# A spectral mixer in fp32 on one core: the first pair of token tiles of a feature phase is combined before it is turned and turned in 32x32 squares, and sums, weight steps and second-layer weights stand at other places

## The chip, the core and the metric

The kernel runs on one core of a Trainium2 chip. Each core has TensorE for matmuls (PE; its weight loads are PEld), VectorE (DVE), ScalarE (ACT), GpSimd (POOL) and SyncE (SP), which here issues nearly all DMAs. Each engine works through its own instructions in order and waits on semaphores for the others. The metric is the device time of one execution in microseconds (us). The kernel before takes 2624.86 us, the median of three runs (2624.60 to 2625.03).

## What is computed

Two layers, each of a Fourier mixing and an MLP, both behind a layer norm, on 2048 tokens of 576 features, all in fp32:

```python
S, D, F = 2048, 576, 4608
def _A_ref(x, dft_seq_re, dft_seq_im, dft_hid_re, dft_hid_im):
    a = jnp.einsum("bsd,ed->bse", x, dft_hid_re)
    b = jnp.einsum("bsd,ed->bse", x, dft_hid_im)
    return jnp.einsum("ts,bse->bte", dft_seq_re, a) - jnp.einsum("ts,bse->bte", dft_seq_im, b)
def _B_ref(x, w1, b1, w2, b2):
    y = _layernorm(x, axis=-1)
    h = _gelu(jnp.einsum("bsd,df->bsf", y, w1) + b1)
    return jnp.einsum("bsf,fd->bsd", h, w2) + b2
x = A_x
x = x + _A_ref(_layernorm(x, axis=-1), ...)
x = x + _B_ref(_layernorm(x, axis=-1), B_w1, B_b1, B_w2, B_b2)
x = x + _A_ref(_layernorm(x, axis=-1), ...)
x = x + _B_ref(_layernorm(x, axis=-1), B_w1, B_b1, B_w2, B_b2)
```

## The kernel before, in words

**Parts and products.** An fp32 matrix is kept as two parts, a rounded high part (a ScalarE copy) and the difference to it, the low part (a VectorE or GpSimd subtraction). A product of two such matrices is three matmuls, high by high, high by low and low by high (`PASSES`), all issued in `mm` (L211). Large products are made of seven block products in place of eight (Winograd's scheme), which asks for sums and differences of blocks of both operands ahead of them and of the results behind.

**A layer** is a sequence phase (`Sequence`) and two halves, each of a feature phase (`hidden`) and an MLP (`mlp`), for 8 token tiles of 128 at a time. So there are four feature phases; the first is that of layer 0, half 0, and is the only one whose feature matrix is not yet split (`made` is false).

**Sequence phase.** A tile t of output (14 of them, two more are made ahead) is seven steps, one for each block product, 24 matmuls of 288 columns each. Around step n, written in one loop (`run`): VectorE makes the low part of step n+2 (`low`), with two updates of blocks in place; ScalarE makes the high part of step n+3; behind the matmuls of step n come its sums out of the accumulators (`post`), and at the last step VectorE turns the result in squares (L208). `sums(t + 1)` adds two blocks into a spare one and updates a third in place for the next tile; it stands at n % 7 = 2. The blocks come by DMA (in_cs, 512 KB) into a ring of six, so block 3 of tile t+1, one of the two that `sums` adds first, is loaded when block 0 of tile t is given back in the first step of tile t.

**Weights in the background.** In layer 0 a generator (`weights`) splits the first-layer weights: ScalarE's high parts (L284, L285), VectorE's low part (128 x 3 x 128), GpSimd's differences of blocks, and a store. `pump` runs one piece of it. `run` pumps twice a step, but for step 2 of a tile; the MLP of the first half goes on at the places in `BEHIND`. The generator is finished in that half.

**Feature phase.** For n = 0 to 7: 54 matmuls, whose first operand is token tile n, loaded, and split by `turn(n)` a step ahead. VectorE adds the result to the tile (L198), the layer norm's statistics follow (L226 to L234, with a power function on GpSimd, L232), and ScalarE normalizes (L238, L258) into a slot of two tiles (`t8`), a pair j. For pairs 0, 1 and 2, behind n = 2, 4 and 6, `rests` copies the remainder of the columns (L977), and `turn_blocks` turns four blocks on TensorE: 8 transposes (L991) and 4 of the remainders (L994), with two ScalarE copies out of the accumulators (L995, L996). In the step behind, `turn_sums` makes the first parts (L1004 and differences) and four differences of the turned blocks, `turn_parts` the parts of those, all into the MLP's operand `y`. The last pair is summed unturned, and `turn_y` turns its seven blocks on TensorE.

**MLP.** 18 chunks of 49 wide matmuls (`inner`), in groups of two; behind each chunk from group 1 on, a part of the second product of the group before (`outer`, 96 or 72 matmuls). A chunk accumulates in four banks, and the next one in the other four. In the first half of layer 0 the second-layer weights are made on the way (`make`): for each group a list of steps at due places, `soon` in the group and `late` in the next one. `advance` runs what is due after each block product, and the pumps.

## Time and profile before

| | us |
|---|---|
| median of three runs | 2624.86 |
| the profiled execution, its own time | 2624.75 |
| its span in the profile | 2623.0 |
| TensorE busy | 2614.4 |
| VectorE busy | 1836.8 |
| ScalarE busy | 1120.2 |
| GpSimd busy | 791.5 |

The page gives the busy time of each engine. Groups of instructions are named by line, engine, operation and tiles, with count, busy time, and mean duration in ns of one. A row of the timeline starts with its start in us and its length; "x4" is the number of instructions merged in it, and what stands in brackets is the engine's idle time ahead, with the instruction that ended it. A row of the chain that ended last has start, length, and engine with line. In a table of stretches a row is a stretch of the span with its length, the busy time of PE, PEld, DVE, ACT and POOL in it with the number of instructions, the granted clock, the busy share of the DMA engines and GB/s.

### The profile page before, as it was taken

The page shows a single profiled execution, that of the slowest core. Times are in us where ns is not written, and L with a number is a line of the kernel's source. Part 1 is how long each engine was busy: PE and PEld are TensorE (multiplying, and loading weights), DVE is VectorE, ACT ScalarE, POOL GpSimd, SP SyncE. Part 2 cuts the span into 40 slices and gives each one's busy share as a digit, 9 for nine tenths or more (in the row PEclk, how much of TensorE's full clock was granted, in tenths as well). Part 3 has the DMA queues.
Part 4 walks back from the last instruction along what each step waited for, and adds up shares of the span by engine and source line. Part 5 has one row for each costly group of instructions (what it writes and reads, how often), then busy time and mean ns, then how long its engine had stood idle before and what let it go on. Part 6 is the DMA issues. An engine that isn't in the chain of part 4 may idle for free.

```text
span 2623.0 us, 44794 instructions
## 1 busy us (share of the span) xinstructions
PE 2614.4 (100%) x17252; PEld 2466.3 (94%) x17252; DVE 1836.8 (70%) x2580; ACT 1120.2 (43%) x1821; POOL 791.5 (30%) x638
## 2 busy tenths in 40 slices
PE   9999999999999999999999999999999999999999
PEld 9999999899999989998999999999999999899998
DVE  8999987778787765556687776576555557655555
ACT  7555555555553443333354333353333325433332
POOL 5334333544444332222251000132122233322222
PEclk9999999999999999999999999999999999999999
DMA  6667676778788666676544343756666685666664
GB/s 226 223 236 234 234 255 215 266 278 301 279 299 300 178 202 195 194 222 210 173 175 135 122 124 124 211 159 194 193 195 194 195 268 169 199 195 195 194 194 155
DMA packets 223238, 544.91 MB, mean 208 GB/s; under 512 B 23712, under 2 KB 74912, under 8 KB 222880
## 3 DMA queue, kind: packets, MB, share of 16 engines
q1 hardware_dynamic: 210496, 513.91, 62.2%
q10 hardware_dynamic: 12528, 28.12, 2.8%
q8 instruction: 137, 2.24, 0.3%
q14 instruction: 77, 0.63, 0.1%
HBM read 429.87 MB, written 114.72 MB: 208 GB/s over the span
## 4 chain that ended last, share of the span: by engine, by line
PE 92%; DVE 5%; DMA 1%; issue 1%; POOL 1%; ACT 0%; DVEq 0%; ACTq 0%; SPq 0%; POOLq 0%
PE bank L211 91%; DVE R L201 3%; DVE A L201 1%; DMA w_parts<-R 1%; DMA A<-in_cs 0%; PE bank L991 0%; DVE A L198 0%; PE bank L1035 0%; DVE moments L242 0%; PE bank L994 0%; ACT R L698 0%; DMA A<-in_w 0%; DMA R<-w_parts 0%; PE bank L1045 0%; POOL A L198 0%
## 5 line engine op out<-in xcount | busy, mean ns | idle before, releaser
L211 PE MATMUL bank<-R 128*128 128x288 f32 (+2 forms) x16972 | 2585.9, 314 | 3.9 <-DVE R L201 1.2
L211 PEld LDWEIGHTS bank<-R 128*128 128x128 f32 x16972 | 2434.8, 189 | 150.8 <-DVE R L201 4.3
L198 DVE TENSOR_TENSOR A<-bank,A 128x576 f32<-128x576 f32 (+3 forms) x812 | 567.6, 707 | 510.2 <-PE bank L211 457.7
L201 POOL TENSOR_TENSOR R<-A,R 128x512 fp32r<-128x512 f32 (+1 forms) x292 | 380.0, 1310 | 912.4 <-ACT R L1299 560.6
L201 DVE TENSOR_TENSOR R<-A,R 128x1024 fp32r<-128x1024 f32 (+10 forms) x534 | 535.0, 1028 | 34.6 <-ACT R L698 14.3
L1299 ACT ACTIVATE R<-A 128x512 fp32r<-128x512 f32 x288 | 177.5, 630 | 356.4 <-DVE A L201 219.5
L198 POOL TENSOR_TENSOR A<-A 128x576 f32<-128x576 f32 (+2 forms) x102 | 155.0, 1527 | 531.1 <-ACT A L743 338.9
L1234 ACT ACTIVATE bank<-bank,b1t 128x512 f32<-128x512 f32 (+1 forms) x224 | 144.9, 647 | 350.5 <-DVE bank L198 233.6
L698 ACT ACTIVATE R<-A 128x1024 fp32r<-128x1024 f32 x196 | 205.6, 1054 | 123.8 <-PE bank L211 61.0
L198 DVE TENSOR_TENSOR bank<-bank,A 128x512 f32<-128x512 f32 (+1 forms) x228 | 152.3, 670 | 147.7 <-PE bank L211 147.0
L201 POOL TENSOR_TENSOR A<-A 128x288 f32<-128x288 f32 (+3 forms) x152 | 190.3, 1255 | 198.1 <-DVE R L201 103.6
L201 DVE TENSOR_TENSOR A<-A 128x1024 f32<-128x1024 f32 (+3 forms) x166 | 163.5, 989 | 6.2
L201 DVE TENSOR_TENSOR R<-bank,R 128x512 fp32r<-128x512 f32 x232 | 156.1, 676 | 5.5 <-ACT R L1299 5.0
L1299 ACT ACTIVATE R<-bank 128x512 fp32r<-128x512 f32 x216 | 121.0, 595 | 33.9 <-PE bank L211 33.9
L201 DVE TENSOR_TENSOR A<-bank,A 128x512 f32<-128x512 f32 x144 | 98.1, 681 | 0.4
L1261 ACT ACTIVATE A<-bank 128x512 f32<-128x512 f32 (+1 forms) x76 | 43.7, 575 | 120.2 <-PE bank L211 120.1
L284 ACT ACTIVATE R<-A 128x256 fp32r<-128x256 f32 x126 | 51.9, 412 | 63.7 <-DMA w_parts<-R 27.1
L1234 ACT ACTIVATE A<-bank,b1t 128x512 f32<-128x512 f32 (+1 forms) x76 | 50.5, 665 | 63.4 <-DVE bank L198 63.4
L232 POOL TENSOR_TENSOR moments<-moments,power 128x1 f32<-128x1 f32 x32 | 25.5, 797 | 134.9 <-DVE moments L234 117.5
L285 ACT ACTIVATE R<-A,power,middle 128x128 fp32r<-128x128 f32 x126 | 60.6, 481 | 0.0
L258 ACT ACTIVATE A<-A,moments 128x576 f32<-128x576 f32 x58 | 49.3, 867 | 23.7 <-DMA A<-x_mid 11.7
L198 DVE TENSOR_TENSOR A<-A 128x1024 f32<-128x1024 f32 x28 | 35.8, 1277 | 20.0 <-DMA A<-in_cs 12.3
(70 smaller groups left out, 612.9 us busy)
## 6 DMA issues: line engine op xcount, KB each, us to landing
R<-w_parts SPq DMA_DIRECT2D x504, 320.0 KB, 3.4
R<-w_parts SPq DMA_DIRECT2D x189, 576.0 KB, 3.7
A<-in_cs SPq DMA_DIRECT2D x112, 512.0 KB, 4.5
w_parts<-R SPq DMA_DIRECT2D x63, 576.0 KB, 6.2
w_parts<-R ACTq DMA_DIRECT2D x75, 320.0 KB, 4.3
w_parts<-R SPq DMA_DIRECT2D x51, 320.0 KB, 4.9
uv_mid<-A SPq DMA_DIRECT2D x28, 576.0 KB, 5.4
A<-in_w SPq DMA_DIRECT2D x72, 192.0 KB, 5.4
```

What stands on the lines that cost most here:

```text
L198: engine.tensor_tensor(dst, a, b, op=op)
L201: engine.tensor_tensor(dst, a, b, op=OP.subtract)
L211: nc.tensor.matmul(o, a, b, start=start, stop=stop, skip_group_check=True)
L232: nc.gpsimd.tensor_tensor(mv[:, 3:4], mv[:, 2:3], power[:, 0:1], op=OP.pow)
L258: nc.scalar.activation(dst, src, AF.Identity, bias=mv[:, 4:5], scale=mv[:, 3:4])
L284: nc.scalar.activation(t[:, 1:4:2], src[:, 0:3:2], AF.Copy)
L285: nc.scalar.activation(t[:, 2], src[:, 1], AF.Identity, bias=power[:, 2:3], scale=middle)
L698: nc.scalar.activation(self.cells[t, i](2, NP, P)[:, 0], self.source(t, i), AF.Copy)
L1234: nc.scalar.activation(dst, src, AF.Gelu_apprx_tanh, bias=bias(f))
L1261: nc.scalar.activation(up, o, AF.Copy)
L1299: nc.scalar.activation(H[q, k](2, TC)[:, 0], src, AF.Copy)
```

## The change

It has three parts. In the sequence phase, `sums` is taken apart: the addition stands at step 3, the update at step 4, and the step without pumps is step 6; in the last tile pumps go on for longer. In the first MLP half, the first four steps of group 0's `late` list move into group 0 (`due` at 5, 6, 12 and 13), `BEHIND` has other places, and group 1 has its own list with two pumps less (`BEHIND_1`). And in the three later feature phases (`flip`) the first pair is not turned by TensorE: ScalarE normalizes it into a mixed order of columns (`mixed`), VectorE makes the four differences unturned and turns all seven blocks in squares of 32 (`turn_first`), `move_first` writes them to DRAM (`y_mid`) and reads them back with the squares at their places, and `first_parts` makes the parts late in step 4.

```diff
--- before.py
+++ after.py
@@ -62,7 +62,9 @@
 EXTRA_AT = 7424
 EARLY_X = (12800, 9344, 8192)
 EARLY_T = 10496
-BEHIND = (0, 2, 2, 4, 5, 6, 15, 16, 16, 17, 17, 19, 21, 21)
+BEHIND = (0, 2, 4, 4, 6, 6, 15, 16, 17, 17, 19, 19, 21, 21)
+FIRST_AT, FIRST_K = 10464, 6
+BEHIND_1 = (0, 2, 4, 4, 15, 16, 17, 17, 19, 19, 21, 21)
 H_AT = (8704, 22400)
 C2_AT = (OWN_AT, 37760)
 Y_AT = (RN - Y_N, 0)
@@ -176,6 +178,7 @@
     dhp = nc.dram_tensor("dh_parts", (KH, P, 2, D), F32, kind="Internal").ap()
     uvd = nc.dram_tensor("uv_mid", (NT, P, 2 * D), F32, kind="Internal").ap()
     w1s = nc.dram_tensor("w1_parts", (NQ, 7, P, 5 * P), F32, kind="Internal").ap()
+    yd = nc.dram_tensor("y_mid", (P, 4, 3, 7 * 32), F32, kind="Internal").ap()
     w2s = nc.dram_tensor("w2_parts", (NG, 7, P, 2, 2 * DH), F32, kind="Internal").ap()
     ctx.enter_context(tc.manual_schedule())
 
@@ -685,9 +688,11 @@
         def block(self, t, k):
             return self.live[t, k](NP, P)
 
-        def sums(self, t):
-            add(nc.vector, self.tmp(NP, P), self.block(t, 2), self.block(t, 3))
-            sub(nc.vector, self.block(t, 2), self.block(t, 2), self.block(t, 0))
+        def sums(self, t, which=(0, 1)):
+            if 0 in which:
+                add(nc.vector, self.tmp(NP, P), self.block(t, 2), self.block(t, 3))
+            if 1 in which:
+                sub(nc.vector, self.block(t, 2), self.block(t, 2), self.block(t, 0))
 
         def source(self, t, i):
             return self.tmp(NP, P) if i == 5 else self.block(t, {1: 0, 6: 0, 2: 1, 7: 2, 3: 1, 4: 3}[i])
@@ -772,8 +777,8 @@
                 self.load_c()
                 if n and n + 2 < len(steps):
                     self.low(*steps[n + 2])
-                if n % 7 == 2 and t + 1 < NT:
-                    self.sums(t + 1)
+                if n % 7 in (3, 4) and t + 1 < NT:
+                    self.sums(t + 1, (n % 7 - 3,))
                 self.load_c()
                 if n + 3 < len(steps):
                     self.high(*steps[n + 3])
@@ -790,7 +795,7 @@
                     hidden.begin(self, ORDER.index(i))
                 if n == 3 and not self.early:
                     dma(b1t, b1)
-                if n % 7 != 2 and n > 3 and (t < NT - 1 or n % 7 < 4):
+                if n % 7 != 6 and n > 3 and (t < NT - 1 or n % 7 < 5):
                     pump()
                     pump()
             for k in range(2):
@@ -943,7 +948,7 @@
         t8s = Slots(A, 2, 8 * DH)
         es, b2t = A.alloc(7 * 3 * 32, low=True), A.alloc(D, low=True)
         dma(b2t(D), b2.to_broadcast([P, D]))
-        t8 = {}
+        t8, flip, first_x = {}, h.made, []
 
         def norms(n):
 
@@ -957,7 +962,12 @@
             yield
             if n < NP - 1:
                 shift(mv)
-                normalize(z, tile_x, mv)
+                if flip and n < 2:
+                    xg = tile_x.rearrange("p e (g i) -> p e g i", i=32)
+                    for e, k in enumerate((0, 1) if n else (3, 2)):
+                        normalize(mixed()[:, k], xg[:, e], mv)
+                else:
+                    normalize(z, tile_x, mv)
             else:
                 nc.vector.tensor_scalar(z, tile_x, mv[:, 0:1], mv[:, 3:4], op0=OP.subtract, op1=OP.mult)
                 b12, b22, b11, b21 = (v[:, k] for k in range(4))
@@ -970,6 +980,50 @@
             if n < NP - 1:
                 add(nc.gpsimd, tile_x, tile_x, b2t(2, DH))
             yield
+
+        def mixed():
+            return t8[0](8 * DH).rearrange("p (g e i) -> p e g i", e=8, i=32)
+
+        def turn_first():
+            b12, b22, b21, b11, t1, t3, t2, t4 = (mixed()[:, k] for k in range(8))
+            sub(nc.vector, t1, b12, b11)
+            sub(nc.vector, t3, b22, b12)
+            sub(nc.vector, t2, b22, t1)
+            sub(nc.vector, t4, b21, t2)
+            v = t8[0](9, 8 * 32)[:, :, 32:]
+            nc.vector.transpose(v, v)
+
+        def move_first():
+            v = t8[0](9, 8 * 32)[:, :, 32:]
+            for f in range(2):
+                dma(yd[:, :, f], v[:, 4 * f:4 * f + 4])
+            dma(yd[:, :, 2], v[:, 8:9].to_broadcast([P, 4, 7 * 32]))
+            t8s.give(t8.pop(0))
+            for f0, f1, b in ((0, 3, A.place(FIRST_AT, 12 * 7 * 32)),) if half else (
+                    (0, 2, R.place(0, 8 * 7 * 32)), (2, 3, R.place(C1_AT[0], 4 * 7 * 32))):
+                first_x.append((f0, f1, b))
+                x, src = b(4, (f1 - f0) * 7 * 32), yd[:, :, f0:f1].rearrange("(q d) c f x -> c d q (f x)", q=4)
+                for c in range(4):
+                    to = x[32 * c:32 * c + 32]
+                    dma(to if half else to.bitcast(F32), src[c])
+
+        def first_parts():
+            at = slice(0, P)
+            for f0, f1, b in first_x:
+                x = b((f1 - f0) * 4 * 7 * 32)
+                x = (x if half else x.bitcast(F32)).rearrange("p (q f i t) -> p f i q t", q=4, i=7, t=32)
+                for f in range(f0, f1):
+                    yf = y[:, :, f, at].rearrange("p i (q t) -> p i q t", q=4)
+                    nc.scalar.activation(yf, x[:, f - f0], AF.Copy)
+            for f0, f1, b in first_x:
+                x = b((f1 - f0) * 4 * 7 * 32)
+                x = (x if half else x.bitcast(F32)).rearrange("p (q f i t) -> p f i q t", q=4, i=7, t=32)
+                for f in range(f0, f1):
+                    part = slice(64, 96) if f == 2 else slice(0, P)
+                    yf, to = (y[part, :, k, at].rearrange("p i (q t) -> p i q t", q=4) for k in (f, 2 if f == 2 else 3 + f))
+                    sub(nc.vector, to, x[part, f - f0], yf.bitcast(F32))
+            for _, _, b in first_x:
+                b.free()
 
         def rests(j):
             v = t8[j](8, DH)
@@ -1055,8 +1109,12 @@
             if n:
                 drain(turn(n + 1))
                 next(ln)
-            if n >= 2 and n % 2 == 0:
+            if flip and n == 2:
+                turn_first()
+            elif n >= 2 and n % 2 == 0:
                 rests(n // 2 - 1)
+            if flip and n == 3:
+                move_first()
             if n == NP - 3:
                 next(mlp)
             o = space()
@@ -1069,10 +1127,12 @@
             for k in range(KH):
                 if n == 0 and k == KH // 2:
                     drain(turn(1))
-                if n in (3, 5) and k == 2:
+                if n in (3, 5) and k == 2 and (n == 5 or not flip):
                     turn_sums((n - 3) // 2)
                 if k == 4:
                     next(ln, None)
+                if flip and n == 4 and k == FIRST_K:
+                    first_parts()
                 for m, (a, b) in enumerate(PASSES):
                     for e in range(2):
                         mm(o[:, e, :DH], u(2, KH, P)[:, a, k], h.dd[k][b](2, DH)[:, e],
@@ -1083,9 +1143,11 @@
             add(nc.vector, tile_x, o[:, :, :DH], tile_x)
             ln = norms(n)
             next(ln)
-            if n in (3, 5):
+            if n == 5 or n == 3 and not flip:
                 turn_parts((n - 3) // 2)
-            if n >= 2 and n % 2 == 0:
+            if flip and n == 2:
+                h.ring += 2
+            elif n >= 2 and n % 2 == 0:
                 turn_blocks(n // 2 - 1)
             if n == NP - 2:
                 turn_sums(2)
@@ -1194,7 +1256,7 @@
 
         def advance(to=None):
             at[1] += to is None
-            for _ in range(BEHIND.count(at[0]) if to is None and group[0] else 0):
+            for _ in range((BEHIND if group[0] > 1 else BEHIND_1).count(at[0]) if to is None and group[0] else 0):
                 pump()
             while kept and kept[0][0] <= at[1]:
                 kept.pop(0)[1]()
@@ -1380,10 +1442,11 @@
         for k in range(4 * first):
             load_raw(0, k)
         for g in range(NG + 1):
-            at[0], group[0] = 0, g or not first
+            at[0], group[0] = 0, g if first else NG
             if first and not g:
                 soon, late = make(0)
-                due.extend((n, step) for n, (_, step) in zip((3, 4), soon))
+                due.extend((n, step) for n, (_, step) in zip((3, 4, 5, 6, 12, 13), soon + late[:4]))
+                late = late[4:]
             elif first:
                 due.extend(late)
                 if g < NG:
```

**VectorE in a tile of layer 0's sequence phase.** The rows of before start behind the low part of step 2, the first of tile 4: "128x3x128" is a low part of the background weights, "R<-A,R 128x1024" the low part of a step, "A<-A 128x1024" an update or a sum of blocks, "bank" a sum out of the accumulators.

```order
L201 TENSOR_TENSOR R<-A,R 128x1024 [waits DMAHW5_49,Activation_49]
L201 TENSOR_TENSOR A<-A 128x1024 [waits DVE_49]
L201 TENSOR_TENSOR R<-A,R 128x3x128 [waits DMAHW3_49,Activation_49,Pool_49]
L201 TENSOR_TENSOR R<-A,R 128x1024 [waits Activation_49]
L198 TENSOR_TENSOR A<-bank,A 128x288 [waits PE_49,Activation_49]
L201 TENSOR_TENSOR R<-A,R 128x3x128 [waits DMAHW5_49,DMAHW1_49,Activation_49]
L201 TENSOR_TENSOR R<-A,R 128x1024 [waits Activation_49]
L198 TENSOR_TENSOR A<-A 128x1024 [waits DMAHW7_49,DMAHW0_49,DVE_49]
L201 TENSOR_TENSOR A<-A 128x1024 [waits DMAHW6_49,DVE_49]
L201 TENSOR_TENSOR R<-A,R 128x1024 [waits Activation_49]
L201 TENSOR_TENSOR R<-A,R 128x3x128 [waits DMAHW6_49,DMAHW4_49]
L201 TENSOR_TENSOR R<-A,R 128x1024 [waits PE_49,Activation_49]
```

And the same tile in the changed kernel, from the same instruction on:

```order
L204 TENSOR_TENSOR A<-A 128x1024 [waits DVE_49]
L204 TENSOR_TENSOR R<-A,R 128x3x128 [waits DMAHW2_49]
L204 TENSOR_TENSOR R<-A,R 128x1024 [waits Activation_49]
L201 TENSOR_TENSOR A<-bank,A 128x288 [waits PE_49,Activation_49]
L204 TENSOR_TENSOR R<-A,R 128x3x128 [waits DMAHW3_49,Activation_49,Pool_49]
L204 TENSOR_TENSOR R<-A,R 128x1024 [waits Activation_49]
L204 TENSOR_TENSOR R<-A,R 128x3x128 [waits DMAHW4_49,DMAHW1_49,Activation_49]
L204 TENSOR_TENSOR R<-A,R 128x1024 [waits DVE_49,Activation_49]
L201 TENSOR_TENSOR A<-A 128x1024 [waits DMAHW5_49,DMAHW0_49,DVE_49]
L204 TENSOR_TENSOR R<-A,R 128x3x128 [waits DMAHW7_49,DMAHW6_49,Activation_49]
L204 TENSOR_TENSOR R<-A,R 128x1024 [waits PE_49,Activation_49]
L204 TENSOR_TENSOR A<-A 128x1024 [waits DVE_49]
```

The addition (L198 before, L201 now, with two DMA waits) stood behind the low part of step 4 with the update right after it; now a weight step and the low part of step 5 come ahead of it, and another weight step and the low part of step 6 between it and the update.

**TensorE in the feature phase of layer 0, half 1.** Before, from the end of the MLP half ahead of it:

```order
L211 MATMUL bank<-R 128x512 x49
L211 MATMUL bank<-R 128x288 x402
L991 MATMUL bank<-ident,A 128x128 x8
L994 MATMUL bank<-ident,A 96x128 x4
L211 MATMUL bank<-R 128x288 x108
L991 MATMUL bank<-ident,A 128x128 x8
L994 MATMUL bank<-ident,A 96x128 x4
L211 MATMUL bank<-R 128x288 x108
L991 MATMUL bank<-ident,A 128x128 x8
L994 MATMUL bank<-ident,A 96x128 x4
```

In the changed kernel, at the same place:

```order
L214 MATMUL bank<-R 128x512 x49
L214 MATMUL bank<-R 128x288 x510
L1045 MATMUL bank<-ident,A 128x128 x8
L1048 MATMUL bank<-ident,A 96x128 x4
L214 MATMUL bank<-R 128x288 x108
L1045 MATMUL bank<-ident,A 128x128 x8
L1048 MATMUL bank<-ident,A 96x128 x4
```

The first group of 8 and 4 transposes is gone; what was 402 and 108 matmuls on its two sides is one run of 510.

**The queue of SP and VectorE in that part.** SP in the changed kernel, layer 0, half 1, from the loads of tile 5 (uv_mid, in_x) to the first MLP weights (w_parts):

```order
L198 DMA R<-uv_mid 32x4x288 x4
L198 DMA A<-in_x 128x2x288
L198 DMA y_mid<-A 512x1x224 x3
L198 DMA A<-y_mid 32x4x672 x4
L198 DMA R<-uv_mid 32x4x288 x4
L198 DMA A<-in_x 128x2x288
L198 DMA R<-uv_mid 32x4x288 x4
L198 DMA A<-in_x 128x2x288
L198 DMA R<-w_parts 128x640 x7
```

The three writes and four reads of `y_mid` are new, between the loads of tile 5 and those of tile 6. VectorE in the last feature phase, around the sum of tile 4 out of the accumulators ("bank"), before:

```order
L234 TENSOR_SCALAR moments<-moments 128x1
L201 TENSOR_TENSOR R<-A,R 32x4x128 [waits Activation_49]
L201 TENSOR_TENSOR R<-A,R 128x4x2x128
L201 TENSOR_TENSOR R<-R 128x1152 [waits DMAHW6_49,DMAHW1_49,DMAHW7_49,DMAHW0_49,Activation_49]
L198 TENSOR_TENSOR A<-bank,A 128x2x288 [waits DMAHW5_49,PE_49]
L226 BN_STATS moments<-A 128x6 [waits DVE_49,Pool_49]
```

and in the changed kernel:

```order
L204 TENSOR_TENSOR R<-R 128x1152 [waits DMAHW2_49,DMAHW1_49,DMAHW3_49,DMAHW0_49,Activation_49]
L204 TENSOR_TENSOR R<-A,R 128x7x128 [waits DMAHW2_49,DMAHW1_49,DMAHW3_49,DMAHW0_49,Activation_49]
L204 TENSOR_TENSOR R<-A,R 128x7x128 [waits Activation_49]
L204 TENSOR_TENSOR R<-A,R 32x7x128 [waits Activation_49]
L201 TENSOR_TENSOR A<-bank,A 128x2x288 [waits DMAHW7_49,PE_49]
L229 BN_STATS moments<-A 128x6 [waits DVE_49,Pool_49]
```

The three differences of `first_parts` ("128x7x128", "32x7x128") now stand between the low part of tile 5 ("R<-R 128x1152") and the sum of tile 4; before, the second half of pair 0's parts stood ahead of that low part.

## The prediction

> **What bounds the kernel now.** I read the busy times first, then the chain that ended last, then stretches of the span cut at the program's own steps.
>
> ```profile
> PE 2614.4 (100%) x17252; PEld 2466.3 (94%) x17252; DVE 1836.8 (70%) x2580; ACT 1120.2 (43%) x1821; POOL 791.5 (30%) x638
> PEclk9999999999999999999999999999999999999999
> 1294.80 407.37 PE bank L211 x3078
> ```
>
> TensorE is busy all the time at full clock, so only two things can shorten the span: fewer TensorE instructions, or fewer stalls between them. A "busy" TensorE may still be stalled, so I compare stretches with the same matmuls. The third row, from the chain in order of time, is a stretch without a stall: 407.37 us for 3078 matmuls, 132.4 ns each, so a tile of the sequence phase (7 steps of 24 matmuls, 168) needs 22.2 us. Now the same tiles in layer 0, in a table of stretches cut at tile starts (stretch, length, then busy time of PE, PEld, DVE, ACT, POOL):
>
> ```profile
> 104.66:126.87 22.21, 22.21 (x170) 22.21 (x169) 21.71 (x21) 12.56 (x23) 9.59 (x6) 1.00 0.76 235
> 149.27:172.67 23.40, 22.81 (x170) 22.35 (x169) 21.75 (x22) 12.88 (x23) 6.58 (x5) 1.00 0.66 229
> 195.68:219.07 23.39, 22.73 (x171) 22.35 (x169) 20.49 (x22) 12.80 (x24) 8.02 (x6) 1.00 0.68 232
> 308.45:331.35 22.90, 22.76 (x171) 22.31 (x170) 21.75 (x24) 13.05 (x24) 7.04 (x5) 1.00 0.67 235
> sum 315.89, PE 314.21 PEld 311.81 DVE 297.92 ACT 178.58 POOL 110.76; mean PE 22.44 PEld 22.27 DVE 21.28 ACT 12.76 POOL 7.91
> ```
>
> Fourteen tiles at 22.21 us would be 310.94; they take 315.89, so **4.95 us** are stalls, most of them in the three tiles quoted with over 22.9 and in one like them. VectorE has 21 to 22 us of work in a tile of 22.2, so whatever it waits for comes out as a TensorE stall. The other place is the first MLP half of layer 0:
>
> ```profile
> 452.02:475.89 23.87, 23.17 (x100) 18.33 (x99) 17.14 (x28) 15.52 (x30) 10.35 (x9) 1.00 0.84 273
> 475.89:489.74 13.85, 13.04 (x97) 12.81 (x96) 9.09 (x13) 5.16 (x10) 7.64 (x7) 1.00 0.69 252
> 489.74:501.68 11.94, 11.54 (x52) 9.16 (x50) 11.24 (x16) 8.62 (x18) 7.39 (x6) 1.00 0.57 186
> 511.24:522.54 11.30, 11.30 (x51) 9.25 (x50) 10.04 (x12) 5.88 (x12) 8.07 (x7) 1.00 0.79 272
> 522.54:535.28 12.74, 12.74 (x98) 12.74 (x97) 10.93 (x17) 5.67 (x11) 5.61 (x6) 1.00 0.88 322
> ```
>
> A chunk of the inner product (49 wide matmuls) needs 11.30 and an outer part of 96 needs 12.74, as the last two rows show. The first rows hold two chunks, one outer part and one chunk: 23.87 - 22.60, 13.85 - 12.74 and 11.94 - 11.30 give 1.27 + 1.11 + 0.64 = **3.02 us** of stalls.
>
> **The transposes that go.** One group of the kind removed, from the chain in order of time:
>
> ```profile
> 2171.69 0.87 PE bank L991 x8
> 2172.56 0.44 PE bank L994 x4
> 2173.00 14.40 PE bank L211 x108
> 2203.10 0.87 PE bank L991 x8
> ```
>
> 0.87 + 0.44 = 1.31 us, three times: **-3.93 us** of TensorE. It counts fully, unless a wait takes its place.
>
> **What takes their place.** I work it out in the last feature phase, in the clock of the rows. The first group stands at the end of token tile 2 (2171.69). A tile is 54 matmuls, 14.40 / 2 = 7.2 us, so without the group tile 3 ends at 2178.9, tile 4 at 2186.1, and, with the second group (1.31), tile 6 at 2201.8.
>
> ```profile
> 2168.54 1.36 DVE L201 TENSOR_TENSOR R<-R 128x1152 fp32r<-128x1152 f32 x1 [1.85 <-DMA R<-uv_mid]
> L201 DVE TENSOR_TENSOR A<-A 128x288 f32<-128x288 f32 x16 | 6.6, 454 | 0.3
> L208 DVE STREAM_TRANSPOSE A<-A 128x1152 f32<-128x1152 f32 x32 | 44.1, 1377 | 2.9
> R<-uv_mid SPq DMA_DIRECT2D x12, 144.0 KB, 3.0
> w_parts<-R SPq DMA_DIRECT2D x51, 320.0 KB, 4.9
> R<-dh_parts SPq DMA_DIRECT2D x23, 576.0 KB, 8.7
> ```
>
> VectorE is free for the new work at 2169.9. Four differences at 0.45 and the transpose of 9 x 224 = 2016 columns at 1377 x 2016 / 1152 = 2.4 us end at 2174.1. Three writes of 448 KB and then the reads follow on SP. A write of 320 KB lands in 4.9 us (the median of its kind) and a read of 144 KB in 3.0; for three and four issues and the larger size I take 6 + 5 us, nearest to those rows, so the turned blocks are back at about 2185. The ends are 2 x 3.0 (2180) and 2 x 8.7 (2191.5). SP waits ahead of the reads, and the loads for tile 6 stand behind them; they land some 5 us later than now, which is still ahead of ScalarE's copy of them behind tile 4.
>
> The new reader is three ScalarE copies and three VectorE differences late in tile 4, and **VectorE's sum of tile 4 out of the accumulators stands behind them**.
>
> ```profile
> 1699.33 0.87 ACT L258 ACTIVATE A<-A,moments 128x576 f32<-128x576 f32 x1
> 1700.23 0.52 ACT L977 ACTIVATE A<-A 128x384 f32<-128x384 f32 x1
> L596 ACT ACTIVATE R<-A 128x864 fp32r<-128x864 f32 x15 | 13.9, 927 | 0.4
> L201 DVE TENSOR_TENSOR R<-A,R 128x864 fp32r<-128x864 f32 x16 | 18.0, 1127 | 2.7 <-ACT R L596 2.7
> 1695.00 0.76 DVE L198 TENSOR_TENSOR A<-bank,A 128x576 f32<-128x576 f32 x1 [2.82 <-PE bank L211]
> 2187.43 0.76 DVE L198 TENSOR_TENSOR A<-bank,A 128x576 f32<-128x576 f32 x1
> 2201.43 0.87 ACT L258 ACTIVATE A<-A,moments 128x576 f32<-128x576 f32 x1
> ```
>
> In the earlier phase ScalarE was through with a tile's normalization and remainder 5.75 us after that tile's sum (1695.00 to 1700.75). After the sum of tile 3 at 2179.0 that is 2184.7, about when the data arrive. Copies of 128x896 cost 0.93 to 0.96, differences 1.1 to 1.17: VectorE is through at 2185.0 + 0.95 + 3.3 = 2189.2, and the sum of tile 4, ready at 2186.2, comes 3.0 us late. In the profile the normalization of tile 5, which the third group of transposes needs, ends 2202.30 - 2187.43 = 14.9 us after that sum, through VectorE and ScalarE without a gap to speak of; now it ended 0.8 us before the group (2203.10). From 2189.2 it ends at 2204.1, when TensorE has been ready since 2201.8: a stall of **2.3 us where 1.31 was saved**. The two transposes of the group that need only tile 4 can run meanwhile (0.2). Per phase that is +0.8, and +2.4 for three. Bounds: -3.9 (nothing is late) and, with 8.7 us each way and so 6.5 us more in each phase, +2.4 + 19.5 = +21.9; the landings nearby are far from that end.
>
> **The sums moved (tile t+1's, from step 2 to 3 and 4).**
>
> ```profile
> 158.17 0.33 SPq L195 DMA_DIRECT2D A<-in_cs  x1
> A<-in_cs SPq DMA_DIRECT2D x112, 512.0 KB, 4.5
> 162.81 1.23 DVE L198 TENSOR_TENSOR A<-A 128x1024 f32<-128x1024 f32 x1 [1.15 <-issue]
> 209.18 1.23 DVE L198 TENSOR_TENSOR A<-A 128x1024 f32<-128x1024 f32 x1 [2.08 <-issue]
> ```
>
> Issued at 158.17, a block lands at 162.67; the sum starts at 162.81 after 1.15 us of idle VectorE. The row says "issue", but it is this DMA. In the worst tile it is 2.08. One step later is 3.2 us later, so these waits go. The step behind the tile's end, which has the turn (1.38) and two updates, loses a weight difference too, since the pump now skips step 6 and not 2. What is late next is VectorE's own work. I take **-4.2** of the 4.95. Bounds: -4.95 and 0 (VectorE is 21.71 / 22.21 = 98% full, and the stalls only move).
>
> **The MLP's second-layer weights made earlier, fewer pumps in group 1.**
> ```profile
> L201 DVE TENSOR_TENSOR R<-A,R 128x576 fp32r<-128x576 f32 x63 | 53.4, 847 | 0.1
> L201 DVE TENSOR_TENSOR R<-A,R 128x384 fp32r<-128x384 f32 x126 | 100.4, 797 | 0.0
> ```
>
> In the second chunk of the stretch from 452.02, VectorE loses two weight differences of 0.85 and one of 0.80, 2.5 of its 17.14 us over both chunks, and that where TensorE waited for it; ScalarE loses the copies to them. They move into the first chunk, whose matmuls have the other four banks, so TensorE covers them; what may stall there is ScalarE, in order behind a GpSimd difference that the second copy needs. I take **-1.9** of 3.02, bounds -3.0 and +0.5. The other halves' pumps find nothing left to do: 0.
>
> **Sum.** Against this execution's 2624.75 us (span 2623.0 and 1.75 around it; the median of the runs is 2624.86): +2.4 - 4.2 - 1.9 = -3.7, hence **2621.1 us**.
>
> **Rivals.**
> - *The new work hides.* Data back by 2182 and VectorE through before tile 4 ends: -3.9 - 4.2 - 1.9 = -10.0, 2614.8. For it: DMA is idle there, and VectorE has slack in tile 3. Against: ScalarE's own position gives 2184.7 at the earliest. Chance 0.22.
> - *The sequence stalls only move.* VectorE has as much work as before: +2.4 - 1.0 - 1.9, 2624.3. Against: the tile from 104.66 has no stall at 21.71 us of work, the one from 149.27 has 1.2 at 21.75. 0.13.
> - *GpSimd's power function is blocked.* With its sum late, VectorE runs into the next difference right behind the statistics.
>
> ```profile
> 2189.69 0.55 POOL L232 TENSOR_TENSOR moments<-moments,power 128x1 f32<-128x1 f32 x1 [0.99 <-DVE moments L234]
> 1697.10 1.36 DVE L201 TENSOR_TENSOR R<-A,R 128x1152 fp32r<-128x1152 f32 x1
> 1697.13 1.75 POOL L232 TENSOR_TENSOR moments<-moments,power 128x1 f32<-128x1 f32 x1 [1.70 <-DVE moments L234]
> ```
>
> Where that difference starts first, the function takes 1.75 us, not 0.55: +1.2 in the chain of each phase, +3.6, 2624.7. [...] 0.15.
> - *Slower: the way through DRAM is late.* Beyond 2185 each microsecond costs one in each of three phases. At 2188.0 that is +9.0, from where the kernel is slower by 0.2%; with 8.7 us each way (2191.5) it is +19.5, 2640.6. Against: that landing time is of crowded stretches. 0.05.
>
> **How the numbers follow.** The forecast has 0.45. A measurement tells about 0.2%, 5.2 us, from no change: 2619.6 to 2630.1 is "same". A fifth of the forecast's chance lies below 2619.6: faster 0.22 + 0.09 = 0.31; slower 0.05; same 0.64. The range for 8 in 10 leaves out the slow tail and the lowest tenth: 2614.5 to 2626.0.
>
> **What would show it.** Right: groups of 12 transposes left at the second and third place only; TensorE idle for some 2 us ahead of the third, released by ScalarE's normalization; no idle VectorE ahead of the sums and tiles of 22.2 us in layer 0; 98 wide matmuls in 22.6 to 23. Wrong: no idle ahead of the third group (the first rival), tiles still over 23, or a stall after tile 4 on the loads for tile 6.

## The result, and the profile after

The changed kernel takes 2650.9 us (median of 5 runs, 2648.07 to 2653.42), the kernel before beside it 2625.01 (2624.60 to 2625.85): a ratio of 1.010 with an interval of 1.0088 to 1.0112. It is 26 us slower, where 3.7 us faster was forecast. The profiled execution took 2650.41 us, its span is 2648.6, 25.6 more than before. The page's first lines hardly show it:

```profile
PE 2617.6 (99%) x17216; PEld 2467.9 (93%) x17216; DVE 1836.2 (69%) x2574; ACT 1113.0 (42%) x1818; POOL 798.3 (30%) x638
```

TensorE has 36 instructions fewer and is busy 3.2 us longer. So, as before, stretches with the same matmuls. This is the table of stretches of the changed kernel: first the 14 tiles of layer 0's sequence phase, then pieces of the MLP's first half, cut where a row of matmuls of one width begins.

```profile
60.46:373.65 313.19, 311.89 (x2354) 311.19 (x2353) 289.93 (x293) 178.42 (x320) 111.83 (x72) 1.00 0.66 235
449.96:475.28 25.32, 23.48 (x100) 18.27 (x100) 18.09 (x27) 15.25 (x29) 14.14 (x12) 1.00 0.92 303
499.28:510.31 11.03, 9.84 (x74) 9.63 (x73) 7.82 (x12) 4.63 (x10) 2.67 (x2) 1.00 1.04 403
636.98:648.04 11.06, 9.80 (x74) 9.60 (x73) 7.82 (x12) 4.56 (x9) 2.64 (x2) 1.00 1.01 388
1029.32:1038.88 9.56, 9.56 (x74) 9.56 (x73) 7.11 (x11) 3.53 (x6) 1.58 (x2) 1.00 0.55 186
```

The sequence phase went from 315.89 to 313.19, **-2.7**. The first two chunks of the MLP went from 23.87 to 25.32, and the outer parts of 72 matmuls, which run in 9.56 us in the second half (the last row), take up to 11.06. Nine outer parts (seven of 72 matmuls, two of 96) are slow; with the first chunks the stalls of this half are 11.0 us where they were 3.0, **+8.0**. And the end of the last feature phase: tiles 5 and 6 (108 matmuls), the third group of transposes with its wait, tile 7 (54 matmuls), first before, then after:

```profile
2188.48:2202.94 14.46, 14.46 (x112) 14.46 (x110) 12.03 (x23) 9.06 (x12) 3.79 (x5) 1.00 0.68 219
2202.94:2204.17 1.23, 1.23 (x15) 1.23 (x13) 1.07 (x3) 0.10 (x1) 1.23 (x1) 1.00 0.36 62
2204.17:2211.44 7.27, 7.27 (x57) 7.27 (x55) 5.78 (x13) 3.81 (x6) 2.23 (x3) 1.00 0.47 153
...
2204.65:2221.38 16.73, 14.86 (x111) 14.55 (x110) 10.65 (x18) 7.49 (x10) 3.11 (x2) 1.00 0.87 253
2221.38:2228.61 7.23, 2.43 (x14) 2.15 (x12) 6.91 (x13) 4.79 (x6) 3.01 (x2) 0.73 0.26 82
2228.61:2237.21 8.60, 8.60 (x57) 8.60 (x56) 5.73 (x12) 3.44 (x6) 2.06 (x2) 0.83 0.21 70
```

That is 9.6 us more than before here. The same pieces of the two other phases were 8.8 and 5.8 us longer; less 3 x 1.23 for the groups that went, the feature phases lost **20.4**. The sum, -2.7 + 8.0 + 20.4 = 25.7, is the 25.6 of the span.

The granted clock, the third number from the right, is new: 0.73 and 0.83. In the page's 40 slices it doesn't show, since it fell to one half for 3 to 7 us only. How the wait came about is seen in rows of the timeline of VectorE, SP, ScalarE and TensorE there:

```profile
2187.37 2.91 DVE L204 TENSOR_TENSOR A<-A 128x288 f32<-128x288 f32 x4
2190.31 2.28 DVE L994 STREAM_TRANSPOSE A<-A 128x2016 f32<-128x2016 f32 x1
2192.65 2.05 SPq L198 DMA_DIRECT2D y_mid<-A  x3
2198.39 1.73 SPq L198 DMA_DIRECT2D A<-y_mid  x4
2206.76 2.64 ACT L1017 ACTIVATE R<-A 128x896 fp32r<-128x896 f32 x3 [4.08 <-DMA A<-y_mid]
2207.75 3.21 DVE L204 TENSOR_TENSOR R<-A,R 128x896 fp32r<-128x896 f32 x3 [7.35 <-ACT R L1017]
2210.99 0.76 DVE L201 TENSOR_TENSOR A<-bank,A 128x576 f32<-128x576 f32 x1
2214.57 6.91 PE L214 MATMUL bank<-R 128*128 128x288 f32 x50 [1.87 <-DVE R L204]
2221.83 0.75 DVE L201 TENSOR_TENSOR A<-bank,A 128x576 f32<-128x576 f32 x1
2225.58 0.87 ACT L261 ACTIVATE A<-A,moments 128x576 f32<-128x576 f32 x1
2226.50 1.54 PE L1045 MATMUL bank<-ident,A 128*128 128x128 f32 x6 [4.80 <-ACT A L261]
```

Tile 4 ended at 2203.4, its sum came at 2210.99, 7.6 us late. TensorE then waits twice: 1.87 us for the low part of tile 6, which stands behind that sum on VectorE, and 4.80 us at the third group for the normalization of tile 5.

### The profile page after: what moved, and what is told of

It is laid out like the page before. It is cut to its first block, busy times and chain, and to the rows that moved or that the text cites. A ratio compares the mean times of both kernels' runs of the same rounds, so it can differ in the third digit from the quotient of the medians.

```text
span 2648.6 us, 44760 instructions
## 1 busy us (share of the span) xinstructions
PE 2617.6 (99%) x17216; PEld 2467.9 (93%) x17216; DVE 1836.2 (69%) x2574; ACT 1113.0 (42%) x1818; POOL 798.3 (30%) x638
## 4 chain that ended last, share of the span: by engine, by line
PE 75%; DMA 3%; DVE 2%; ACT 1%; POOL 1%; issue 1%; SPq 0%; ACTq 0%; DVEq 0%; POOLq 0%
PE bank L214 74%; DMA w_parts<-R 1%; DMA R<-uv_mid 1%; DVE R L204 1%; ACT R L1361 1%; DVE A L204 0%; DMA R<-w_parts 0%; DVE A L201 0%; POOL moments L235 0%; POOL A L201 0%; SPq L198 0%; DMA A<-y_mid 0%; PE bank L1089 0%; DMA A<-x_mid 0%; DVE moments L229 0%
## 5 line engine op out<-in xcount | busy, mean ns | idle before, releaser
L201 DVE TENSOR_TENSOR A<-bank,A 128x576 f32<-128x576 f32 (+3 forms) x812 | 568.2, 707 | 510.1 <-PE bank L214 463.2
L204 DVE TENSOR_TENSOR R<-A,R 128x1024 fp32r<-128x1024 f32 (+9 forms) x522 | 522.7, 1024 | 74.1 <-ACT R L703 27.3
L201 POOL TENSOR_TENSOR A<-A 128x576 f32<-128x576 f32 (+2 forms) x102 | 150.5, 1482 | 532.4 <-ACT A L748 344.0
L1296 ACT ACTIVATE bank<-bank,b1t 128x512 f32<-128x512 f32 (+1 forms) x224 | 144.4, 645 | 342.4 <-DVE bank L201 227.0
L201 DVE TENSOR_TENSOR bank<-bank,A 128x512 f32<-128x512 f32 (+1 forms) x228 | 152.3, 670 | 146.2 <-PE bank L214 145.4
L287 ACT ACTIVATE R<-A 128x256 fp32r<-128x256 f32 x126 | 52.1, 413 | 128.1 <-DMA w_parts<-R 90.0
L235 POOL TENSOR_TENSOR moments<-moments,power 128x1 f32<-128x1 f32 x32 | 35.9, 1122 | 150.9 <-DVE moments L237 128.8
L1296 ACT ACTIVATE A<-bank,b1t 128x512 f32<-128x512 f32 (+1 forms) x76 | 50.6, 665 | 62.7 <-DVE bank L201 62.7
L261 ACT ACTIVATE A<-A,moments 128x576 f32<-128x576 f32 (+1 forms) x64 | 51.0, 820 | 23.9 <-DMA A<-x_mid 12.0
L204 DVE TENSOR_TENSOR A<-A,bank 128x512 f32<-128x512 f32 x72 | 48.8, 677 | 0.0
```

The lines of the kernel that those rows point to most:

```text
L201: engine.tensor_tensor(dst, a, b, op=op)
L204: engine.tensor_tensor(dst, a, b, op=OP.subtract)
L235: nc.gpsimd.tensor_tensor(mv[:, 3:4], mv[:, 2:3], power[:, 0:1], op=OP.pow)
L261: nc.scalar.activation(dst, src, AF.Identity, bias=mv[:, 4:5], scale=mv[:, 3:4])
L287: nc.scalar.activation(t[:, 1:4:2], src[:, 0:3:2], AF.Copy)
L1296: nc.scalar.activation(dst, src, AF.Gelu_apprx_tanh, bias=bias(f))
```

## Experiments

Ratios are to the kernel before, run on the same chip in between, with a 95% interval. Waits and lengths of stretches are from one profile each.

**Which of the three parts costs.** The turned blocks taken out of the changed kernel, and put alone into the kernel before:

```diff
-        t8, flip, first_x = {}, h.made, []
+        t8, flip, first_x = {}, False, []
```

> The turned blocks and the way through DRAM are off in all feature phases, as in the kernel before; the moved sums, the new places of the weight preparation and the earlier second-layer steps stay. Theory: the 25.6 us that the changed kernel's span lost are about 20 in the feature phases, about 8 in the first half of layer 0's MLP, and minus 2.7 in layer 0's sequence phase, and the three are independent: 2650.9 - 20 = 2630 to 2631 us, the MLP's 72-matmul outer parts still 9.8 to 11.1 us where 9.56 is the pace, no granted clock of 0.5 before the end. Rival: the MLP's loss comes from the memory places and DMA traffic of the turned blocks: it goes too, about 2622 us.

2633.35 us, 1.0033 (1.0021 to 1.0044). Six outer parts of 72 matmuls still take 10.6 to 11.0 us; the feature phases are back at the lengths of before within 0.02 us, and the clock is at 1.0 until the end. The other way round, with the turned blocks as the only edit:

> The kernel before with the turned blocks of the three feature phases alone; sums, preparation and second-layer steps as before. Theory: they cost the same alone, 17 to 20 us by the stages of the changed kernel's profile: 2641 to 2645 us, with waits of 4 us and more at the third transposing group. Rival: the loss needs the other edits: under 2635 us.

2642.88 us, 1.0066 (1.0052 to 1.0080): 17 to 18 us (in its profile the feature phases lose 19.3, and the 14 tiles of the sequence phase are 2.4 shorter than in the one profile before), and in the MLP's first half the stalls of before, none of the new ones. So the two losses are apart.

**The MLP: the order within a place.**

```diff
-BEHIND = (0, 2, 4, 4, 6, 6, 15, 16, 17, 17, 19, 19, 21, 21)
-BEHIND_1 = (0, 2, 4, 4, 15, 16, 17, 17, 19, 19, 21, 21)
+BEHIND = (0, 2, 2, 4, 5, 6, 15, 16, 16, 17, 17, 19, 21, 21)
+BEHIND_1 = (0, 2, 2, 4, 5, 6, 15, 17, 17, 19, 21, 21)
```

> The places at which the MLP of layer 0's first half prepares first-layer weights are those of before (in the first group less one difference and one store, since the sequence phase now makes two steps more); all else as changed. Theory: the loss comes from a store and the next piece's difference and copy standing at one place, so that ScalarE's copy waits for the store that was issued just ahead of it (3.6 us at 502.96): the outer parts go back to about 9.6 us, 5 to 6 us less, about 2645 us. Rival: the loss comes from the second-layer steps that were moved into the first group: no change, 2650 to 2651 us.

2643.55 us, 1.0073 (1.0056 to 1.0090). The second run keeps the changed places and adds one step:

```diff
-BEHIND_1 = (0, 2, 4, 4, 15, 16, 17, 17, 19, 19, 21, 21)
+BEHIND_1 = (0, 2, 4, 4, 5, 15, 16, 17, 17, 19, 19, 21, 21)
```

> The new places stay, with one preparing step more in the first group, so that at every place with two steps the difference and copy come first and the store second. Theory (the order within a place): the outer parts go back to about 9.6 us, about 2645 us, as with the places of before. Rival (the places themselves, 17, 19 and 21 with two steps each beside the second-layer work): no change, 2650 to 2651 us, the 72-matmul parts still 9.8 to 11.1 us.

2645.65 us, 1.0078 (1.0063 to 1.0093). In both, every outer part is within 0.6 us of its pace. Steps come by turns: one stores piece n, the next makes the low part of n+1 and the high part of n+2, into the ring place that piece n-1 left (the ring has three). A group has 14 steps, so the number made before it decides, for all groups, which of the two comes first at a place with two. The changed kernel, on SP and ScalarE (L302 is the store, L287 the high part, L1296 the activation for which the matmuls' banks wait):

```profile
497.20 0.61 SPq L302 DMA_DIRECT2D w_parts<-R  x1
500.22 0.81 SPq L302 DMA_DIRECT2D w_parts<-R  x1
502.96 0.42 ACT L287 ACTIVATE R<-A 128x256 fp32r<-128x256 f32 x1 [3.62 <-DMA w_parts<-R]
503.67 0.64 ACT L1296 ACTIVATE bank<-bank,b1t 128x512 f32<-128x512 f32 x1
506.96 5.29 PE L214 MATMUL bank<-R 128*128 128x288 f32 x32 [1.20 <-ACT R L1361]
```

and with one step more:

```profile
494.47 0.32 SPq L302 DMA_DIRECT2D w_parts<-R  x1
497.89 0.41 SPq L302 DMA_DIRECT2D w_parts<-R  x1
498.38 0.69 ACT L1296 ACTIVATE A<-bank,b1t 128x512 f32<-128x512 f32 x1 [0.90 <-DVE bank L201]
498.97 0.41 ACT L287 ACTIVATE R<-A 128x256 fp32r<-128x256 f32 x1
499.93 0.66 ACT L1296 ACTIVATE bank<-bank,b1t 128x512 f32<-128x512 f32 x1 [0.17 <-DVE bank L201]
```

The copy does not wait for the store just ahead of it, as was expected, but for the one a place earlier: that was issued at 497.20 and landed 5.7 us later, at 502.9, where the copy begins, while the store of 500.22 landed at 506.7. With the store first at every place with two, only one place lies between a store and the copy that refills what it emptied; ScalarE is there 2.1 us after the issue and waits 3.62 us, all behind it waits too, and TensorE for that. With the store last, one place more lies between: the copy at 498.97 needs the store of 494.47, which landed at 497.0, and does not wait. The places themselves are innocent.

**The second-layer steps in group 0.**

```diff
-zip((3, 4, 5, 6, 12, 13), soon + late[:4]))
-                late = late[4:]
+zip((3, 4), soon))
```

> The second-layer weight steps of the MLP's first half go back from the first group to the second, as before; all else as changed. Theory: in the first group GpSimd's difference of a second-layer weight (1.43 us at 463.55) stands ahead of its last difference of the hidden part, so that ScalarE's first copy and then TensorE wait (1.59 us at 466.88): the 98 wide matmuls go from 25.3 us back to about 23.9, the later outer parts stay as they are: 1.4 us less, 2649 to 2650 us. Rival: the two steps at a place wait less for stores when the second-layer steps are out of the way, or more when they come back into the second group: the outer parts change by more than 1 us in sum.

The first two chunks went from 25.32 to 23.89, as the theory has it, but the whole is unchanged: 2651.15 us, 1.0107 (1.0092 to 1.0122). 1.4 us is less than this comparison tells.

**The feature phases: the place, the way through DRAM, the clock.** First the copies and differences moved behind tile 4's sum and statistics:

```diff
-                if flip and n == 4 and k == FIRST_K:
-                    first_parts()
...
             next(ln)
+            if flip and n == 4:
+                first_parts()
```

> In the three feature phases the copies and differences of the first token pair stand behind the sum of tile 4 and its statistics instead of ahead of them; all else as changed. Theory: what costs is that VectorE's sum of tile 4 stands behind work that waits for the DRAM way: the sum goes from 7.6 us late to under 1, the normalization of tile 5 is no longer late by more than 1.5 us, TensorE waits at the third transposing group for 0 to 1.5 us in place of 4.0 to 4.8, the granted clock stays off 0.5, and each phase gets 4 to 6 us back: 2633 to 2639 us. Rival: the DRAM way itself is what is late, and ScalarE's in-order copies hold the following splits just as long: stalls of 3 us or more stay at tile 6 or the third group, 2646 us or more.

2638.91 us, 1.0055 (1.0040 to 1.0070): 12 us less, but the waits at the third group are 2 to 3 us, not under 1.5. ScalarE still stood 4.15 us for the DMA. In the next run it has none: copies and differences read a block that is ready (`x = t8[1](8 * DH)[:, :4 * 7 * 32]`; line numbers are shifted by one there), so this kernel leaves the turned blocks out of its result.

> The copies and differences of the first token pair read another block of the same size in SBUF, which is ready long before, and not what the way through DRAM brings; all transfers and every instruction stay, in their places. The first 128 tokens' parts are so made from other data. It tells the term of the prediction (no wait for DRAM, the work in its place ahead of tile 4's sum) from the lateness. Theory: of the 7.6 and 4.6 us by which the sum of tile 4 was late, the wait for DRAM makes 4.1 and 1.3, the work in the wrong place the rest: the sum is about 3.5 us late, TensorE waits at the third group for 0.5 to 2.5 us, no half clock: 4.5 to 6 us less a phase, 2633 to 2638 us. Rival: the work alone fills the phase: waits of 3.5 us and more and the half clock stay: 2645 us or more.

2636.97 us, 1.0051 (1.0036 to 1.0066). In the last phase:

```profile
2196.72 3.21 DVE L204 TENSOR_TENSOR R<-A,R 128x896 fp32r<-128x896 f32 x3 [3.16 <-ACT R L1018]
2199.96 0.76 DVE L201 TENSOR_TENSOR A<-bank,A 128x576 f32<-128x576 f32 x1
2214.99 1.34 PE L1046 MATMUL bank<-ident,A 128*128 128x128 f32 x6 [1.80 <-ACT A L261]
```

Tile 4 ended at 2197.1: its sum is 2.9 us late (forecast without lateness: 3.0), and TensorE waits 1.80 us at the third group (forecast: 2.3; in the two other phases it waits 2.98 and 1.61 there). The work in that place costs about what was forecast, and the lateness of the data came on top. Then the copies and differences ten microseconds later:

```diff
-                if flip and n == 4 and k == FIRST_K:
+                if flip and n == 6 and k == 2:
```

> The copies and differences of the first token pair stand inside tile 6, some 10 us later than as changed (in the phase of layer 1's first half with the third term in another place of SBUF); all else as changed. Theory (both the place ahead of tile 4's sum and the wait for the way through DRAM are the loss, and both are gone when it is waited for 10 us later): no wait over 0.6 us at tile 6 and the third group, no granted clock of 0.5 ahead of the end, the feature phases at their length of before less 1.2 us each; only the MLP's 8 us stay: 2626 to 2630 us. Rival: 5.9 us of copies and differences are too much for these phases wherever they stand, and the sum of tile 6 or the MLP's first products wait in their place: 2633 us or more.

2650.44 us, 1.0105 (1.0088 to 1.0122): nothing gained. The last phase shows what had stood in the shade of the copies (line numbers are shifted by one here too):

```profile
2209.17 1.17 ACT L208 ACTIVATE R<-R 128x1152 fp32r<-128x1152 f32 x1 [3.40 <-DMA R<-uv_mid]
2221.78 0.88 PE L1046 MATMUL bank<-ident,A 128*128 128x128 f32 x6 [2.57 <-ACT A L262]
2238.38 1.86 PE L1090 MATMUL bank<-ident,A 128*128 128x128 f32 x12 [2.16 <-DVE A L205]
```

The load for tile 6 is late, issued behind the reads, which wait on SP for the writes. With the four reads behind that load (a `read_first` called after `h.load(n + 2)` at n == 4):

> As the run with the copies and differences inside tile 6, and the four reads back from DRAM issued behind the load of the pair sums of tile 6 instead of ahead of it. Theory: there, ScalarE's split of tile 6 waited 3.4 us for that load, which SyncE had issued 4 us late, since it stood behind reads that wait for the writes: with the reads behind it the wait is under 1 us, the third transposing group waits less than 1 us, and only the end of the phase (VectorE's sum of tile 6 behind the differences) is late: 2636 to 2644 us. Rival: the load is late because it shares the 16 DMA engines with the turned blocks (7.3 us to landing against 3.0 elsewhere): it lands as late in any order, 2648 us or more.

2643.37 us, 1.0069 (1.0054 to 1.0085). No wait for the load, and the third groups take 1.23 us in all three phases; the 3 us have gone on to the last transposes (`turn_y`), which wait for VectorE. So the differences were given to GpSimd in tile 6, with ScalarE's copies in the second half of tile 5 and the weights' places and second-layer steps of before:

```diff
-                    sub(nc.vector, to, x[part, f - f0], yf.bitcast(F32))
+                    sub(nc.gpsimd, to, x[part, f - f0], yf.bitcast(F32))
```

> An attempt at a faster version: moved sums kept, weight preparation and second-layer steps as in the kernel before; of the turned blocks the reads behind the load of tile 6, ScalarE's copies in the second half of tile 5, and the three differences on GpSimd in tile 6, so that VectorE has none of them in its order. Theory: VectorE was the engine that had no room for 3.2 us between the sums of tile 4 and tile 6; with its order free the phases are those of before less 1.2 us each: 2616 to 2621 us, no granted clock of 0.5. Rival: GpSimd takes 2 us and more for each difference and holds VectorE or its own power function up: waits of 2 us and more at the third group or at the MLP's first products: 2628 us or more.

2633.56 us, 1.0031 (1.0020 to 1.0043). Up to tile 7 each phase is at its pace, less a group; then TensorE waits again, 3.03 us at `turn_y`:

```profile
2206.30 6.48 POOL L204 TENSOR_TENSOR R<-A,R 128x896 fp32r<-128x896 f32 x3
2208.46 5.60 DVE L204 TENSOR_TENSOR R<-A,R 32x256 fp32r<-32x256 f32 x4 [1.18 <-ACT R L1063]
2221.40 2.82 PE L1094 MATMUL bank<-ident,A 128*128 128x128 f32 x12 [3.03 <-DVE A L204]
```

VectorE's four low parts beside them, 1.86 us in the profile before, took 5.60. Last the clock by itself, with 36 transposes of the identity in the wait:

```diff
+                if flip and j == 2 and n == 1:
+                    for _ in range(FILL):
+                        nc.tensor.transpose(b[:, 1, :P], ident, ident)
```

> 36 transposes of the identity into an unused half of the bank (about 3.7 us by 0.10 us each) stand in the third transposing group behind its first two, where TensorE waits 4.0 to 4.8 us for the normalization of tile 5; all else as changed. Theory: the wait stays, but the granted clock stays at 1.0 behind it, where it was 0.5 for 6.83, 3.41 and 6.83 us; the half clock costs half of that: 17.07 / 2 = 8.5 us at most, 6 to 8.5 us less, 2642.5 to 2645 us. Rival: behind the wait ScalarE and VectorE set the pace and the half clock is hidden: less than 2 us, 2649 us or more.

2645.63 us, 1.0088 (1.0073 to 1.0103). The clock is at 1.0 throughout, and the third group and tile 7 together take 39.5 us in the three phases instead of 45.7: 6.3 us of the 20.4 are the half clock. By the whole time the gain is 3 to 5 us, with an interval wide enough for 6.3 too.

**The sequence phase: one profile was too few.** The runs with both the sums and the preparing steps moved have 312.3 to 314.8 us for the 14 tiles (twelve profiles, mean 313.4), but the turned blocks alone, with the sums as before, have 313.5. So the two halves of this edit and the kernel before were run apart.

> The kernel before with the addition and the update for the next tile at steps 3 and 4, and the preparing steps as before. Theory: VectorE's idle time ahead of the 14 additions (7.9 us in the profile before, 6.4 in that with the turned blocks alone) falls under 1 us by this alone, but TensorE's stalls in the 14 tiles fall by far less than the 4.95 us of the one profile before: the tiles take 312.5 to 314.5 us. Rival (the prediction's term): the idle time was the stalls' cause, the tiles take 311 to 312 us.

> The kernel before with the preparing steps left out at step 6 of a tile and not at step 2, the sums as before. Theory: VectorE's idle time ahead of the additions stays at 5 us or more, the tiles take 313 to 316 us. Rival: this is the edit that takes the stalls away, under 312.5 us.

> The kernel before once more, unchanged, to see how far its 14 tiles of the sequence phase differ from one execution to the next: 315.89 us in the profile before, 313.51 with the turned blocks alone and the same sums. Theory: they differ by 2 us and more between executions, and this one lies between 313 and 316 us. Rival: 315.5 to 316.3 us again, and the turned blocks or their places in memory changed the phase.

The tiles took 311.3 with the sums alone, 313.5 with the preparing steps alone, 314.2 in the kernel before once more. In the groups by line and shape, the number behind the second bar is the engine's idle time ahead of them. For the 14 additions it was 7.9 us before; with the sums alone, and with the steps alone, it is:

```profile
L198 DVE TENSOR_TENSOR A<-A 128x1024 f32<-128x1024 f32 x14 | 17.0, 1214 | 0.0
L198 DVE TENSOR_TENSOR A<-A 128x1024 f32<-128x1024 f32 x14 | 18.7, 1338 | 8.1 <-DVE R L201 4.2 <-DMA A<-in_cs 2.3 <-issue 1.6
```

The page names several releasers, but the wait is the one for the block, as the prediction said: by the landings in the traces, every addition that VectorE was idle for starts 0.08 to 0.12 us behind the landing of an in_cs block, before and with the steps alone.

**A version that beats both.** The sums alone were timed, and beside them a version with a second edit: two steps more in the last tile, so two less in group 1 of the MLP.

> The sums moved alone, timed. Theory: the 14 tiles stay under 312.5 us (311.3 in its one look, 314.3 in the mean of four profiles with the sums as before), 1.5 to 3.5 us off the whole: ratio 0.9987 to 0.9994. Rival: one look was lucky, ratio 0.9996 or more.

> The sums moved, two preparing steps more in the last tile and two less in group 1 of the MLP's first half; steps 2 without preparing steps as before, no turned blocks, second-layer steps as before. Theory: beside the sums' gain, the two stalls behind the first group (1.1 and 1.0 us) go, as they did in the run with all but the turned blocks' and weights' places: 2 us less than the sums alone, ratio 0.9975 to 0.9988. Rival: without the place freed at step 6 the sequence phase gives the gain back: 0.999 or more.

2621.80 us, 0.9989 (0.9980 to 0.9998), and **2620.47 us, 0.9982 (0.9973 to 0.9991)**; the tiles take 311.9 and 311.7. With the sums and the preparing steps both moved, second-layer steps and places as before and no turned blocks, it was 2623.07 us:

> Only the moved sums and preparing steps of layer 0's sequence phase stay; the turned blocks are off, the weight preparation stands at the places of before (one difference and one store less in its first group, since two steps more were made before it), the second-layer steps stand as before. Theory: the three edits are independent, and this is the part that gains: 2.7 us by the first profile of the changed kernel, 2620.5 to 2623 us where before is 2624, ratio 0.9985 to 0.9995. Rival: the gain of the sequence phase is within what its stalls differ by from run to run: 2623.5 us or more, ratio 0.9995 or more.

0.9992 (0.9983 to 1.0000), and the tiles take 313.1: leaving step 6 without preparing steps, in place of step 2, gives part of the gain back. This rests on the tiles; the intervals of the whole times overlap.

## Why the prediction was wrong

- **The transposes that go, -3.93.** Right: no group behind tile 2, 3 x 1.23 = 3.7 us.
- **The new work, +2.4 with the groups taken off; it was +20.4.** This step failed: the wait was right in kind and too small, and the half clock behind it was put at nothing. The wait forms where it was forecast, behind tile 4's sum at the third group, and without the lateness it is 1.80 us where 2.3 was said. What failed is the way through DRAM, "back at about 2185". The transpose was estimated at 2.4 us and took 2.28; the four differences took 2.91, not 1.8; the writes took about the 6 us allowed (2192.65 to 2198.39). But from the first read's issue to the copies it is 8.4 us (2198.39 to 2206.76), where 5 was taken "nearest to those rows": the slow row, 8.7 us for 576 KB, was called a figure of crowded stretches (the DMA share of before is 0.91 to 1.03 where those reads stand, 819 to 840, 1660 to 1684 and 2118 to 2148), and this is one:

```profile
2198.39:2206.76 8.37, 8.37 (x67) 8.37 (x66) 1.75 (x3) 2.11 (x4) 3.84 (x3) 1.00 0.92 201
```

The DMA share, the last number but one, is 0.92 (and in the profile before it was 0.59 from 2170 to 2180, where the first rival called DMA idle). Whether the reads are slow for the other transfers or by their own pattern was not run apart. Together the data are 4.5 us later; 3.0 + 4.5 is about the 7.6 us by which the sum was late.

- **What that lateness costs.** One microsecond each was the rule, and the waits of the last phase follow it: 1.87 + 4.80 = 6.7, by the rule 2.3 + 4.5 = 6.8. That is closer than its parts: 1.1 us of the 6.7 are GpSimd's blocked function (below), which the rule leaves out. What no part of the prediction had is the clock: 6.3 us behind the waits. The slower rival thus named the lateness, with a chance of 0.05; that the term came near its upper bound, +21.9, is luck, since that bound stood for a later landing alone and the clock made 6.3 of it.
- **The load for tile 6**, "still ahead of ScalarE's copy": wrong, but hidden in the changed kernel, where ScalarE is later still. With the copies out of its way, ScalarE waits 3.40 us for it.
- **GpSimd's blocked function** happened (1.68 us for the function at 2213.24, beside VectorE's low part of 1.36 us from 2213.15; 0.55 at 2189.69 before). It was not tried apart; it stands in the chain that ends in the 4.80.
- **The sums, -4.2.** The cause was right, the size not: VectorE's idle time goes, and the sums alone bring the tiles to 311.3 to 311.9. But 315.89 was the slowest of the profiles with the sums as before (314.2 and 313.5 are others), and the steps moved along with them took back about 1.7 of the gain (313.4 against 311.7).
- **The MLP's first half, -1.9, bounds -3.0 and +0.5; it was +8.0.** The step counted what VectorE and ScalarE have to do in the first chunks, and put the later groups at nothing without a reason. It did not read which of two steps at one place comes first, nor how long before a copy the store was issued that frees its ring place. The chain there is ScalarE's wait for that store: 8.3 us over the nine outer parts. The 1.11 and 0.64 us of stalls behind the first two chunks did go; the 1.4 us that came in the chunks are the stall that was named as possible, ScalarE behind a GpSimd difference.

## What to carry to other kernels

Where a list of places feeds a generator of alternating steps, one step more or less upstream changes what stands at every place behind it: print the order for the steady state, and for each step that refills a place compare the time since the store that empties it was issued with that store's landing (here 2.1 us and 5.7). An in-order engine with a late reader in its queue passes the lateness to all that stands behind it (here ScalarE stood 4.08 us for the copies, tile 4's sum came 7.6 us late, and TensorE waited 1.87 and 4.80 us); moving the reader only moves the wait if the engine has no free time before the next deadline (here the wait went from tile 6, 1.87 us, to the third group, 2.87, and on to the last transposes, 2.95). Before a one-profile difference of 2 us is used as a term, see how far a phase differs between two executions of the same kernel.

## What the hardware showed

A short wait of TensorE cost a second time: 6.3 us in the three phases, by the run with the transposes of the identity in it. In the changed kernel the stretches at half clock begin 904.53, 1744.21, 2218.66 and 2641.92 us after the first clock record, which is 265, 511, 650 and 774 times 3.4133 us; they last 6.83, 3.41, 6.83 and, at the run's end, 2.68 us. Successive intervals of such a grid at two places, from the run with the copies behind tile 4's sum; a row's second and third numbers are its length and TensorE's busy time:

```profile
906.70:910.11 3.41, 1.86 (x15) 1.62 (x13) 3.19 (x9) 2.59 (x3) 1.04 (x1) 1.00 0.33 79
910.11:913.52 3.41, 2.12 (x18) 2.12 (x19) 3.31 (x5) 2.88 (x5) 1.98 (x1) 1.00 0.27 105
913.52:916.94 3.42, 3.42 (x28) 3.42 (x28) 2.62 (x9) 2.76 (x5) 1.07 (x2) 1.00 0.02 5
...
2214.00:2217.41 3.41, 1.33 (x12) 1.33 (x13) 3.40 (x4) 2.20 (x5) 2.01 (x2) 1.00 0.46 157
2217.41:2220.83 3.42, 3.42 (x16) 3.42 (x16) 2.64 (x9) 3.35 (x6) 1.22 (x2) 0.50 0.00 0
```

1.86 and 2.12 us of work in an interval left the next at full clock; 1.33 did not (16 matmuls in place of 28). In the changed kernel intervals with 0.92, 0.72 and 0.39 us were followed by half clock and one with 1.63 was not; in the run without the wait for DRAM one with 1.61 (3.41 less the wait of 1.80) was. These few intervals do not fix a border. Of the two waits of about 3 us here (2.84 and 2.87), the one was thus free of a second cost, with 1.55 and 1.29 us of it in two intervals; of the other 2.08 us fell in one.

Beside GpSimd's three differences, 6.48 us, VectorE's four low parts took 5.60 us in place of 1.86: two of the four took 2.33 and 2.52 us, in place of 0.42 and 0.69, about the 2.14 of one GpSimd difference; the other two took 0.43 and 0.28, as before.
